# Rows of V in SBUF at a pitch of 512 bytes in place of 388: an attention kernel on one core

## The chip, the cores and the metric

The kernel runs on one core of one Trainium2 chip. The metric is the time of one execution on the device, in microseconds (us). Most executions of this kernel agree within 0.1%.

## The reference

An attention block whose output is multiplied by a gated feed-forward network. Only the attention matters here: 32 heads, 2048 queries, 2048 keys, 192 columns per head, all in bf16.

```python
scores = jnp.einsum("bhqd,bhkd->bhqk", q, k_cache) * (Dh ** -0.5)
p = _softmax(scores, axis=-1)
o = jnp.einsum("bhqk,bhkd->bhqd", p, v_cache)
# ... o @ wo, and x + s * silu(B(xn))
```

## The kernel before

V of one head is held in a tile of 128 partitions, with 16 rows of V in each. A row has 192 values, a column of ones (its product is the softmax's denominator) and one column of padding: 194 values of 2 bytes, 388 bytes. There are two such tiles, for alternate heads, and V is loaded a head ahead.

```python
vts = [vtp.tile([P, NKT, DH + 2], BF16, name=f"vt{i}") for i in range(2)]   # P=128, NKT=16, DH=192
...
def load_v(h, halves=(0, 1), queue=nc.sync):
    vt = vts[h % 2]
    for t in halves:
        ...                      # head 0 is loaded in two other halves
            nc.sync.dma_start(out=vt[:, :, 0:DH].rearrange("i (p t) d -> i p t d", t=2)[:, :, t, :],
                              in_=A_v_cache[0, h].rearrange("(p i t) d -> i p t d", i=P, t=2)[:, :, t, :])
...
for vt in vts:
    nc.vector.memset(vt[:, :, DH:DH + 1], 1.0)
```

The product with V comes in groups of 16 matmuls. A group belongs to one step p (0 to 7) and uses two rows of V, 2p (t = 0) and 2p + 1 (t = 1). Each pair (r = 0, 1) uses the two halves of the array's rows: in the trace its two matmuls (64 rows x 193 columns each) start 3.4 ns apart in the mean, and one is recorded with 243 ns. So a group is eight pairs: four with the even row, then four with the odd one.

```python
for t in range(2):
    for j in range(4):
        start = p == 0 and t == 0 and j % 2 == 0
        stop = p == NPAIR - 1 and t == 1 and j % 2 == 1
        for r in range(2):
            nc.tensor.matmul(obanks[r][:, j * 256:j * 256 + DH + 1],
                             lhsT=pT2[r * 64:(r + 1) * 64, t * 512 + j * P:t * 512 + (j + 1) * P],
                             rhs=vt[r * 64:(r + 1) * 64, 2 * p + t, 0:DH + 1], start=start, stop=stop)
```

`lhsT` is the stationary operand: beside the 16384 matmuls of this line the trace has 16384 weight loads of pT, of 94 ns each. `rhs`, the row of V, is the moving operand. Before each group stand three rounds of score matmuls (512 columns), and before every eight groups a projection of 20 matmuls. There are 1024 groups.

Of the kernel before, what the change touches and what calls it, by code (L numbers as in the profile page):

```python
# [11 lines left out]
BF16 = mybir.dt.bfloat16  # L12
# [3 lines left out]
P = 128  # L16
DH = 192
# [111 lines left out]
def _kernel_impl(  # L129
# [22 lines left out]
    NKT = SK // P  # L152
# [39 lines left out]
    vtp = att.enter_context(tc.tile_pool(name="vtp", bufs=1))  # L192
# [14 lines left out]
    xnS = xsp.tile([P, DC, SQ], BF16, name="xnS")  # L207
    x_all = fw.tile([P, WX], BF16, tag="xw", name="x_all")
    x_sb = x_all[:, 0:NQT * D].rearrange("p (t d) -> p t d", d=D)
    vts = [vtp.tile([P, NKT, DH + 2], BF16, name=f"vt{i}") for i in range(2)]  # L210
    loads = {}

    def load_x(g, t0=0, t1=4, queue=nc.sync):
# [547 lines left out]
@with_exitstack  # L761
def kernel(
    ctx: ExitStack,
    tc: tile.TileContext,
    A_x: bass.AP,
    A_k_cache: bass.AP,
    A_v_cache: bass.AP,
    A_wq: bass.AP,
    A_wo: bass.AP,
    B_x: bass.AP,  # L770
    B_w1: bass.AP,
    B_w3: bass.AP,
    B_w2: bass.AP,
    out: bass.AP,
):
    _kernel_impl(ctx, tc, A_x, A_k_cache, A_v_cache, A_wq, A_wo, B_w1, B_w3, B_w2, out)
# [30 lines left out]
```

## Time and profile before

The median was 1942.03 us over 3 runs (1940.68 to 1942.1). Six runs that include these have a median of 1941.95 us.

| what | before | where to read it |
|---|---|---|
| TensorE (PE) busy | 1929.6 of 1938.7 us | engines of the page |
| share of the V matmuls in the chain that ended last | 35% | chain of the page |
| V matmuls busy | 851.8 us | groups of the page |
| one V load, issue to landing | 5.6 us | DMA issues of the page |

These lines are from the page of the kernel before. A group's line gives engine, operation, output and inputs, shape, count; then its busy time in us and the mean of one in ns. A queue's line gives packets, MB and its share of the 16 DMA engines. An issue's line ends with the median from issue to landing in us.

```profile
span 1938.7 us, 59672 instructions
PE 1929.6 (100%) x27273; PEld 1318.5 (68%) x27281; DVE 654.0 (34%) x997; ACT 1180.2 (61%) x1278; POOL 282.6 (15%) x501
...
q1 hardware_dynamic: 371136, 125.32, 30.3%
...
PE 98%; DVE 1%; DMA 0%; ACT 0%; issue 0%; POOL 0%; DVEq 0%; ACTq 0%
...
L516 PE MATMUL obank<-vt,pT 64*128 64x193 bf16 x16384 | 851.8, 243 | 0.0
...
vt<-in_A_v_cache_dram SPq DMA_DIRECT2D x63, 384.0 KB, 5.6
```

TensorE is busy for 1929.6 of 1938.7 us, and the chain of waits runs through it for 98% of the span. Anything that makes the time shorter must make TensorE's own stream shorter. V loads are far from critical: they land in 5.6 us and are issued about 50 us before they are used (50.7 us in the median of the trace). One V matmul is recorded with 243 ns in the mean, but most pairs start 82.5 to 83.3 ns after the one before, so several overlap. What counts is the distance from one pair to the next.

### The profile page before, as it was taken

The page shows a single profiled execution, that of the slowest core. Times are in us where ns is not written, and L with a number is a line of the kernel's source. Part 1 is how long each engine was busy: PE and PEld are TensorE (multiplying, and loading weights), DVE is VectorE, ACT ScalarE, POOL GpSimd, SP SyncE. Part 2 cuts the span into 40 slices and gives each one's busy share as a digit, 9 for nine tenths or more (in the row PEclk, how much of TensorE's full clock was granted, in tenths as well). Part 3 has the DMA queues.
Part 4 walks back from the last instruction along what each step waited for, and adds up shares of the span by engine and source line. Part 5 has one row for each costly group of instructions (what it writes and reads, how often), then busy time and mean ns, then how long its engine had stood idle before and what let it go on. Part 6 is the DMA issues. An engine that isn't in the chain of part 4 may idle for free.

```text
span 1938.7 us, 59672 instructions
## 1 busy us (share of the span) xinstructions
PE 1929.6 (100%) x27273; PEld 1318.5 (68%) x27281; DVE 654.0 (34%) x997; ACT 1180.2 (61%) x1278; POOL 282.6 (15%) x501
## 2 busy tenths in 40 slices
PE   9999999999999999999999999999999999999998
PEld 6666666666666666666666666666666666577776
DVE  7333333333333333333333333333333334521111
ACT  6677676767676767776767777677767677210000
POOL 3111111111111111111111111111111110000000
PEclk9999999999999999999999999999999999999999
DMA  7643433323233433353434333434333220937772
GB/s 181 129 101 67 98 68 86 83 60 88 59 89 62 99 62 98 68 162 68 101 65 100 68 101 68 101 64 100 69 71 94 57 69 2 262 67 135 152 152 61
DMA packets 394643, 178.98 MB, mean 92 GB/s; under 512 B 341616, under 2 KB 382832, under 8 KB 394384
## 3 DMA queue, kind: packets, MB, share of 16 engines
q1 hardware_dynamic: 371136, 125.32, 30.3%
q0 software_dynamic: 19472, 45.71, 9.6%
q8 instruction: 215, 3.52, 0.8%
q10 hardware_dynamic: 3776, 4.06, 0.6%
q14 instruction: 44, 0.36, 0.1%
HBM read 52.82 MB, written 27.79 MB: 42 GB/s over the span
## 4 chain that ended last, share of the span: by engine, by line
PE 98%; DVE 1%; DMA 0%; ACT 0%; issue 0%; POOL 0%; DVEq 0%; ACTq 0%
PE obank L516 35%; PE st L487 33%; PE ps L424 14%; PE ps_s L111 11%; PE ps_f L727 3%; PE ps_gu L701 1%; PE st L488 1%; DVE stats L316 0%; PE ps L410 0%; DMA x_all<-in_A_x_dram 0%; DVE xn L346 0%; PE ps L391 0%; PE pst L354 0%; DVE mv L317 0%; PE pk L271 0%
## 5 line engine op out<-in xcount | busy, mean ns | idle before, releaser
L490 ACT ACTIVATE pT<-st 128x1024 bf16<-128x1024 f32 x1024 | 1046.2, 1022 | 251.8 <-PE st L488 236.2
L516 PEld LDWEIGHTS <-pT 64*128 64x128 bf16 x16384 | 713.7, 94 | 242.2 <-ACT pT L490 0.2
L516 PE MATMUL obank<-vt,pT 64*128 64x193 bf16 x16384 | 851.8, 243 | 0.0
L487 PE MATMUL st<-qC,KW 64*128 64x512 bf16 x2046 | 605.6, 376 | 0.1
L525 DVE COPY osum<-obank 128x772 f32<-128x772 f32 x128 | 123.0, 961 | 788.9 <-PE obank L516 788.9
L488 PE MATMUL st<-qB,KW 64*128 64x512 bf16 x1024 | 385.0, 376 | 0.0
L487 PE MATMUL st<-qA,KW 64*128 64x512 bf16 x1022 | 384.3, 376 | 0.4 <-ACT pT L490 0.3
L488 PE MATMUL st<-qC,KW 64*128 64x512 bf16 x1022 | 384.3, 376 | 0.0
L488 PE MATMUL st<-qA,KW 64*128 64x512 bf16 x1022 | 384.3, 376 | 0.0
L487 PEld LDWEIGHTS <-KW 64*128 64x128 bf16 x3068 | 278.0, 94 | 153.8 <-issue 2.1
L424 PE MATMUL ps<-xnT,W 64*128 64x512 bf16 x1280 | 297.2, 376 | 0.0
L424 PE MATMUL ps<-xnS,W 64*128 64x512 bf16 x1280 | 296.3, 376 | 0.0
L488 PEld LDWEIGHTS <-KW 64*128 64x128 bf16 x3068 | 278.0, 94 | 0.7 <-issue 0.6
L377 POOL DMA_DIRECT2D qC<-qA x124 | 65.4, 528 | 1285.6 <-DVE rl_all L532 1270.0
L430 ACT CAST qB<-ps 128x512 bf16<-128x512 f32 x131 | 76.7, 586 | 228.5 <-PE ps L424 222.9
L111 PE MATMUL ps_s<-wo_sb,oT 128*128 128x384 bf16 (+3 forms) x1535 | 208.8, 299 | 0.1
L424 PEld LDWEIGHTS <-W 64*128 64x128 bf16 x2560 | 122.9, 94 | 121.2
L111 PEld LDWEIGHTS <-oT 128*128 128x128 bf16 x1536 | 148.4, 98 | 60.4
L526 DVE TENSOR_TENSOR osum<-osum,obank 128x772 f32<-128x772 f32 x128 | 122.7, 958 | 13.4
L533 DVE TENSOR_TENSOR ostage<-osum,rl_all 128x768 bf16<-128x768 f32 x128 | 122.6, 958 | 4.4
L465 DVE SCALAR_TENSOR_TENSOR hT<-pt,qB 64x512 bf16<-64x512 bf16 x64 | 43.8, 684 | 199.5 <-ACT pt L464 199.5
L429 DVE CAST qA<-ps 128x512 bf16<-128x512 f32 x131 | 90.5, 691 | 25.2 <-PE ps L410 7.3
(84 smaller groups left out, 623.8 us busy)
## 6 DMA issues: line engine op xcount, KB each, us to landing
o_scr<-ostage SPq DMA_DIRECT2D x16, 1536.0 KB, 10.0
vt<-in_A_v_cache_dram SPq DMA_DIRECT2D x63, 384.0 KB, 5.6
qC<-qA POOLq DMA_DIRECT2D x248, 64.0 KB, 1.9
qC<-qB POOLq DMA_DIRECT2D x124, 64.0 KB, 2.3
wo_sb<-in_A_wo_dram POOLq DMA_DIRECT2D x1, 7680.0 KB, 35.3
W<-in_A_wq_dram POOLq DMA_DIRECT2D x32, 160.0 KB, 3.4
W<-in_B_w_dram POOLq DMA_DIRECT2D x32, 80.0 KB, 3.1
W<-in_A_wq_dram POOLq DMA_DIRECT2D x32, 80.0 KB, 2.9
```

What stands on the lines that cost most here:

```text
L111: nc.tensor.matmul(ps[:, 0:w], lhsT=oT[:, k, :], rhs=wo_sb[:, k, c0:c1], start=(k == 0), stop=(k == OC - 1))
L377: nc.gpsimd.dma_start(out=qC[0:64, half, :], in_=qAB[half][64:P, :])
L424: nc.tensor.matmul(ps[:, r * 512:(r + 1) * 512], lhsT=W[rows, j, :], rhs=xs[rows, j // 2, qs], start=(j == 0), stop=(j == 2 * DC - 1))
L429: a = nc.vector.tensor_copy(out=qAB[0][:], in_=ps[:, 0:512])
L430: b = nc.scalar.copy(out=qAB[1][:], in_=ps[:, 512:1024])
L487: nc.tensor.matmul(st2[:, 0:512], lhsT=ka, rhs=qa, start=r == 0 and nr == 3, stop=r == nr - 1)
L488: nc.tensor.matmul(st2[:, 512:1024], lhsT=kb, rhs=qb2, start=r == 0 and nr == 3, stop=r == nr - 1)
L490: nc.scalar.activation(out=pT2[:], in_=st2[:], func=ACT.Exp, scale=att_scale)
L516: nc.tensor.matmul(obanks[r][:, j * 256:j * 256 + DH + 1], lhsT=pT2[r * 64:(r + 1) * 64, t * 512 + j * P:t * 512 + (j + 1) * P], rhs=vt[r ...
L525: nc.vector.tensor_copy(out=osum[:], in_=ov[0])
L526: nc.vector.tensor_tensor(out=osum[:], in0=osum[:], in1=ov[1], op=ALU.add)
L533: nc.vector.tensor_tensor(out=ostage[:, qb * 4:qb * 4 + 4, hg * DH:(hg + 1) * DH], in0=osum[:, :, 0:DH], in1=rl.unsqueeze(2).to_broadcast( ...
```

## The change

Its intent is that each row of V starts on a round address, in the hope that aligned rows stream or land better. The columns in use are the same; only the padding grows. Nothing else is edited, and the order of instructions on all five engines stays the same.

```diff
-    vts = [vtp.tile([P, NKT, DH + 2], BF16, name=f"vt{i}") for i in range(2)]
+    vts = [vtp.tile([P, NKT, 256], BF16, name=f"vt{i}") for i in range(2)]
```

## The prediction

> **What bounds the kernel now.** TensorE. The page gives PE 1929.6 us busy in a span of 1938.7 us; the chain of work that ended last is 98% PE: 35% in the line that multiplies by V (obank<-vt,pT), 33% in the scores, 14% in the projections. The granted clock is 0.999. PE's largest wait is 2.8 us, once, at the start. The other engines have slack: VectorE waits 788.9 us for obank, ScalarE 236.2 us for st.
>
> **How near the V matmuls are to their floor.** They come in groups of 16: eight pairs, each on the two halves of the array's rows. In the timeline the group that starts at 1003.41 us is followed by the next matmul at 1004.08 us; from all records' start times a group takes 669.5 ns in the mean, 83.7 ns a pair. [...] 83.3 ns in the first four pairs, 82.5 in most later ones, 87.5 once in the middle. [...]
>
> **What the change does.** No instruction moves on any engine. V's rows start on multiples of 512 bytes from a tile's base; the tiles above in SBUF move up by 3968 bytes (16 rows x 124 bytes x 2 tiles), keeping their place within 128 bytes. The hope must be that aligned rows stream or land faster.
>
> - Reading. At 388 bytes the 16 rows of a tile start at 16 different offsets within 64 bytes, yet the group's time doesn't depend on the row: the medians for the eight pairs of rows (p = 0 to 7) are all 668 or 669 ns. [...] Expected: 0, at best -3 us.
> - Landing. A V load still consists of 384-byte runs; those take 22 ns in the median, between the 18 of 256-byte and 36 of 768-byte runs, so being unaligned costs nothing visible. A load lands in 5.6 us, issued about 50 us before its use; no PE wait names vt. Faster packets would not shorten the time.
> - The ones column: two memsets of 72 ns, with another step. Nothing.
>
> **Critical path share.** 35% of the span reads V; what the pitch could touch of it is about 0.
>
> **Predicted time.** 1941.5 us, 1935 to 1946 (8 in 10). Faster by over 2%: 0.01; within 2%: 0.97; slower by over 2%: 0.02.
>
> **What would show it.** Unchanged: the V matmuls' busy time (851.8 us) and mean (243 ns), 83 to 84 ns a pair; the chain's shares within a point; V loads landing in about 5.6 us; hardware queue 1 within a point of 30.3%; PE waits under 3 us.
>
> **What would make it wrong.** A power-of-two pitch could put two simultaneous accesses (a pair's reads, a read of V and a weight load from pT, a landing row) in each other's way all the time[...]: pairs well over 84 ns, the V share above 36%. Conversely, if all rows at 388 pay alike for what an aligned row doesn't, pairs fall to 82.5 ns or lower, worth some us. Moved tiles (xnS, W, q, pT) could change scores and projections.

(Cut are what no run of this case shows: a floor for the time of a pair, with the bound on any gain that was worked from it; a way of counting what the read of one row touches; and a half sentence on what 388 bytes do. The sum came to 1941.5 us, with 0 for reading, landing and the column of ones: about 0.5 us below the 1942.03 us of before. The first two cuts take two supports out of it, the bound and one of the two reasons for the 0 of reading; they take no other term. That 0 now stands on the group's time alone, which doesn't depend on the row (668 or 669 ns); "at best -3 us" was the author's estimate.)

## More of the kernel before

The next lines are from the chain that ended last, in order of time (start, us, what). They are two projections, which stand one at every eight V groups; 79 such stretches lie between the two.

```profile
252.21 2.16 PE ps L424 x20
...
1254.52 2.16 PE ps L424 x20
```

So one stretch of eight groups takes (1254.52 - 252.21) / 79 = 12.688 us. This is a finer measure than the span, since the start of the program varies from run to run (the projection at 1254.52 us here is at 1255.22 us in the repeat e1).

## The result, and the profile after

The changed kernel took 1939.39 us in the median of 6 runs (1938.82 to 1939.7), against 1941.95 us of before. The ratio was 0.9988, with a 95% interval of 0.9975 to 1.0001. Ratios here are the mean time of one kernel's runs over that of the other's of the same rounds, so they are not quite the ratio of the medians that are quoted. By the timed runs alone this is "the same", with a gain of about 2 us that the interval doesn't quite separate from zero.

The same parts of the page, after:

```profile
span 1937.4 us, 59668 instructions
PE 1927.5 (99%) x27273; PEld 1316.9 (68%) x27281; DVE 654.4 (34%) x997; ACT 1180.1 (61%) x1278; POOL 282.4 (15%) x501
...
q1 hardware_dynamic: 371136, 125.32, 31.5%
...
PE 98%; DMA 1%; DVE 1%; ACT 0%; SPq 0%; issue 0%; DVEq 0%; ACTq 0%
...
L516 PE MATMUL obank<-vt,pT 64*128 64x193 bf16 x16384 | 849.6, 243 | 0.0
...
vt<-in_A_v_cache_dram SPq DMA_DIRECT2D x63, 384.0 KB, 6.0
```

Two things moved. The V matmuls' busy time fell by 2.2 us, which is about the whole difference of the medians. V's loads became slower: 6.0 us and no longer 5.6, and queue 1 is busier with the same packets and bytes. The 1% of DMA in the chain is not from the change: it is the load of x at the program's start, and a repeat of the kernel before (e1 below) shows it too.

The chain in order of time, after:

```profile
252.66 2.16 PE ps L424 x20
...
1253.72 2.16 PE ps L424 x20
```

A stretch of eight groups takes (1253.72 - 252.66) / 79 = 12.672 us, so 16 ns less, 2 ns per group; 2 ns x 1024 groups are 2 us.

To see where in a group the 2 ns lie, I took the start times of all V matmuls from the trace and averaged, over the groups, the time from one pair's start to the next one's (the last: to the matmul that follows). Of 1021 groups the five that waited for something are left out.

| ns from each pair to the next | 1 | 2 | 3 | 4 | 5 | 6 | 7 | 8 | group |
|---|---|---|---|---|---|---|---|---|---|
| before (388) | 83.3 | 83.3 | 83.3 | 83.3 | 87.5 | 82.5 | 82.5 | 82.8 | 668.7 |
| after (512) | 83.3 | 83.3 | 83.3 | 83.3 | 83.4 | 83.3 | 83.3 | 83.3 | 666.7 |

Pair 5 is the first that uses the odd row of V. Before, it took 4.2 ns more, and the three after it 0.5 to 0.8 ns less each. After, all pairs are alike.

### The profile page after: what moved, and what is told of

Its sections match the earlier page's. It is cut to its first block, busy times and chain, and to the rows that moved or that the text cites. A ratio compares the mean times of both kernels' runs of the same rounds, so it can differ in the third digit from the quotient of the medians.

```text
span 1937.4 us, 59668 instructions
## 1 busy us (share of the span) xinstructions
PE 1927.5 (99%) x27273; PEld 1316.9 (68%) x27281; DVE 654.4 (34%) x997; ACT 1180.1 (61%) x1278; POOL 282.4 (15%) x501
## 3 DMA queue, kind: packets, MB, share of 16 engines
q0 software_dynamic: 19472, 45.71, 10.1%
## 4 chain that ended last, share of the span: by engine, by line
PE 98%; DMA 1%; DVE 1%; ACT 0%; SPq 0%; issue 0%; DVEq 0%; ACTq 0%
PE obank L516 35%; PE st L487 33%; PE ps L424 14%; PE ps_s L111 11%; PE ps_f L727 3%; PE ps_gu L701 1%; DMA x_all<-in_A_x_dram 1%; PE st L488 1%; PE ps L410 0%; DVE stats L316 0%; ACT KW L277 0%; PE pst L354 0%; ACT xnT L356 0%; DVE qA L429 0%; SPq L289 0%
```

## The experiments

There are two questions. What makes pair 5 long at 388 bytes? And what makes the loads slower at 512? Theory A was that the gain lies in the V matmuls themselves; its rival B, that 2 us are the noise of runs and chips. As A held, the next theories were about which property of the pitch counts: where a row starts (its alignment), how near it is to the row below, or how its start differs from that of the row used just before. Twelve runs were made, of which e1 and e2 repeat the two kernels and e9 repeats e7; all were correct. In the text, the "place" of a row is the remainder of its start in bytes, counted from the tile's start, when divided by 16. Where a recorded expectation has a mark of a cut, a clause is out that no run shows. The table at the end of this section has their numbers together.

### e1 and e2: both kernels again

There is no edit; both ran with five rounds on one chip.

> The kernel before, unchanged, against itself: the noise of the comparison. Theory A (the small gain of the change is in the V matmuls themselves: with rows at 388 bytes the second half of each group of 16 costs about 4.5 ns once, and less is given back) expects the same records as in the first profile: a mean of about 669.5 ns from the start of a V group to the next matmul, with the extra 4.5 ns at the second pair of the second half; ratio 1.000. Theory B (the 2 us between the kernels are the chip or the run, not the pitch) expects that this repeat differs from the first profile by as much as the changed kernel did. Packets of 384 bytes: if the mean of 28.5 ns belongs to the kernel it comes again; if it is the chip's, it moves.

> The changed kernel again. Theory A: 666.7 ns in the median from the start of a V group to the next matmul, all pairs alike at 83.3 ns, so faster by 2 ns x 1024 = 2 us, ratio about 0.999 with an interval that excludes 1. Theory B: ratio within 0.0005 of 1. The V loads' slower landing (6.0 us against 5.6, 384-byte packets 33 ns against 28.5 in the mean) comes again if the pitch of 512 bytes causes it.

Measured: 1941.24 us for the kernel before and 1939.44 us for the changed one, with ratios to the runs of before of 0.9998 (0.9984 to 1.0012) and 0.9990 (0.9976 to 1.0003). The V groups came out as the first time to 0.1 ns: 87.5 ns at pair 5 and 668.6 ns a group at 388, 666.7 ns at 512. The packets of 384 bytes of V again took 28.6 ns in the mean at 388 bytes and 33.3 ns at 512, and V landed in 5.6 and 5.8 us. So rival B falls: both effects belong to the kernels. The interval of the timed ratio didn't exclude 1, as A had hoped; the records show the 2 ns, the timed runs of this pair alone only suggest them. The busy time of the group, from the pages of e1 and e2:

```profile
L516 PE MATMUL obank<-vt,pT 64*128 64x193 bf16 x16384 | 851.8, 243 | 0.0
...
L516 PE MATMUL obank<-vt,pT 64*128 64x193 bf16 x16384 | 849.5, 243 | 0.0
```

### e3: a pitch of 392 bytes

```diff
-    vts = [vtp.tile([P, NKT, 256], BF16, name=f"vt{i}") for i in range(2)]
+    vts = [vtp.tile([P, NKT, DH + 4], BF16, name=f"vt{i}") for i in range(2)]
```

> Rows of V at a pitch of 392 bytes, so that each starts on a multiple of 8 bytes, every other one not on a multiple of 16. Theory A in the form that 8 bytes are what counts: groups of 666 to 667 ns as at 512 bytes, ratio about 0.999. Rival: 16 bytes[...] or 512 are needed; then the second half of a group[...] still costs the extra 4.5 ns and the group takes about 669 ns. Landing of V: at 5.6 us if the power-of-two pitch is what slows it, at 6.0 us if not.

Measured: 1940.98 us, ratio 0.9996 (0.9982 to 1.001). Pair 5 took 87.5 ns and a group 668.6 ns, as at 388. That each row starts on a multiple of 8 bytes doesn't help. The packets of V took 28.6 ns, as at 388, and V landed in 5.5 us.

```profile
L516 PE MATMUL obank<-vt,pT 64*128 64x193 bf16 x16384 | 851.9, 243 | 0.0
```

The busy time of the group, from the page of this run, is that of before, 851.8 us.

### e4: a pitch of 512 bytes, each row 4 bytes later

```diff
+    V0 = 2
-                nc.sync.dma_start(out=vt[:, :, 0:DH].rearrange(...      # and so for head 0
+                nc.sync.dma_start(out=vt[:, :, V0:V0 + DH].rearrange(...
-        nc.vector.memset(vt[:, :, DH:DH + 1], 1.0)
+        nc.vector.memset(vt[:, :, V0 + DH:V0 + DH + 1], 1.0)
-                                     rhs=vt[r * 64:(r + 1) * 64, 2 * p + t, 0:DH + 1], start=start, stop=stop)
+                                     rhs=vt[r * 64:(r + 1) * 64, 2 * p + t, V0:V0 + DH + 1], start=start, stop=stop)
```

> Pitch 512 bytes, but every row starts 4 bytes later, so that no row starts on a multiple of 8 bytes. If each row off 8 bytes cost something, all eight pairs would be long: groups well over 670 ns. If the cost is one of going from an aligned to an unaligned stream, it is paid once at the second pair of the group (4.5 ns) and the following pairs take 82.5 ns: groups of 665 to 670 ns. If alignment has no part in it and only a pitch of a power of two has, 666.7 ns as at 512. Time within 3 us of before in all cases. Landing of V as in the changed kernel if the pitch sets it, as before if alignment does.

Measured: 1939.30 us, ratio 0.9988 (0.9975 to 1.0002); all eight pairs 83.3 ns, 666.7 ns a group. V landed in 6.0 us, with packets of 33.1 ns.

```profile
L517 PE MATMUL obank<-vt,pT 64*128 64x193 bf16 x16384 | 849.4, 243 | 0.0
...
vt<-in_A_v_cache_dram SPq DMA_DIRECT2D x63, 384.0 KB, 6.0
```

Here no row starts on a multiple of 8 bytes, and the matmuls are as fast as with aligned rows. So the alignment of each row for itself has no part in the gain, and the loads are as slow as with aligned rows. What the change was meant for, aligned rows, is not what gave the 2 us.

### e5 and e6: the two loops of a group swapped, at 388 and at 512

```diff
-        for t in range(2):
-            for j in range(4):
+        for j in range(4):
+            for t in range(2):
```

The row of V now changes at each of the eight pairs (even, odd, even, ...), and no longer once.

> The kernel before (pitch 388) with the two loops of a V group swapped, so that the row of V changes at each of the eight pairs (seven changes) and no longer once. The group of eight pairs took 669 ns with one change and 666.7 ns where the change costs nothing (pitch 512). Theory C (each change from a row to the one that starts right behind its end costs something): about 2 to 4.5 ns per forward change, so a group of 675 to 685 ns and 6 to 16 us more in all. Theory D (the cost is paid once per group, whatever the order): 669 ns, time as before.

> The same swap with the pitch of 512 bytes. Theory C and D both expect 666.7 ns a group, since a change of row cost nothing at this pitch, and a time as the changed kernel's (1939.4 us). If this one is slower as well, changing the row costs something at any pitch and it was only hidden by the order. The difference to the run with 388 bytes is the worth of the pitch where the row changes often.

Measured: at 388 bytes 1947.72 us, ratio 1.0035 (1.0018 to 1.0051), so clearly slower than before; at 512 bytes 1939.47 us, ratio 0.9993 (0.9976 to 1.0009). The pairs of e5 take 83.3, 87.5, 82.5, 86.2, 82.5, 86.1, 82.5 and 86.1 ns, 676.8 ns a group; those of e6 are all 83.3 ns.

The busy time of the group, from the pages of e5 and e6:

```profile
L516 PE MATMUL obank<-vt,pT 64*128 64x193 bf16 x16384 | 857.7, 243 | 0.0
...
L516 PE MATMUL obank<-vt,pT 64*128 64x193 bf16 x16384 | 849.5, 243 | 0.0
```

The chain of e5 in order of time, to be read as that of before:

```profile
254.24 2.16 PE ps L424 x20
...
1260.24 2.16 PE ps L424 x20
```

A stretch takes (1260.24 - 254.24) / 79 = 12.734 us, 62 ns more than after. Theory C held and D fell: the cost comes with each change from the even row to the odd one. At 512 bytes a change of row is free (83.3 ns at each pair of e6). This pair of runs also amplifies the effect to where timing alone shows it: 1947.72 - 1939.47 = 8.3 us. The changes back, from the odd row to the even one, show no cost; those pairs take 82.5 ns, as do the pairs without a change of row that follow the long pair in the kernel before. In this run the rounds of score matmuls that follow also take 215.0 to 215.2 ns and not 215.8, so a part of the delay is made up afterwards: the groups grew by 10.1 ns against those of e6 (10.3 us in all), the time by 8.3 us.

### e7, e8 and e10: pitches of 448, 516 and 400 bytes

The edit of e3 with 224, 258 and 200 values in the tile's row. Each ran once.

> Pitch 448 bytes, a multiple of 64 but of no larger power of two; a row begins 62 bytes behind the end of the one below. If nearness to the last row's end is what cost the 4.5 ns (388: 2 bytes behind, 392: 6 bytes), the group takes 666.7 ns; if only a pitch that is a multiple of 128 or more avoids it, 669 ns. Landing of V and the mean of its packets: 5.6 us and 28.5 ns if the power of two slows them, 6.0 us and 33 ns if any wide gap does.

> Pitch 516 bytes, just off the power of two: rows start off multiples of 8 bytes as with 388, but 130 bytes behind the end of the row below. Nearness: 666.7 ns a group. Multiple of 64, 128 or 512 bytes needed: 669 ns. Landing of V: 5.6 us if the power of two is what slows it, 6.0 us if a wide gap does.

> Pitch 400 bytes: two rows of a group are at the same place within 16 bytes, but not within 32 or 64. Theory F ([...]388, 392 and 516 change that place, 448 and 512 don't, and a common offset of 4 bytes doesn't) expects no extra time[...] (666.7 ns a group, and no pair of 87.5 ns)[...]. A rival by which only the gap of bytes between rows counts (14 bytes here, 2 and 6 before) expects the same extra time as at 392.

(Theory F is that a V matmul takes longer when its row starts at another place than the row used just before. It left open by which number of bytes the place counts: 16, or 32 or 64, for which it expected the long pair at 400 bytes as well, about 669 ns a group.)

Measured: at 448 and 400 bytes all pairs 83.3 to 83.4 ns and 666.7 ns a group; at 516 bytes 85.8 ns at pair 5, then 82.5, 82.5 and 82.9, and 667.1 ns a group. The single times were 1938.91 (448), 1940.97 (516) and 1938.94 us (400). That of 516 is not the groups' alone: in its trace the first stretch of eight groups, at the program's start, took 1.1 us more than usual, and the median stretch is 12.675 us, 3 ns above the 12.672 of 512.

```profile
L516 PE MATMUL obank<-vt,pT 64*128 64x193 bf16 x16384 | 849.6, 243 | 0.0
...
vt<-in_A_v_cache_dram SPq DMA_DIRECT2D x63, 384.0 KB, 5.4
...
L516 PE MATMUL obank<-vt,pT 64*128 64x193 bf16 x16384 | 850.3, 243 | 0.0
...
vt<-in_A_v_cache_dram SPq DMA_DIRECT2D x63, 384.0 KB, 5.3
```

The first two lines are from the page of e10: the busy time is that of the changed kernel, the landing faster than both. The last two are from that of e8 (516). Nearness alone falls as a theory: at 516 bytes the odd row begins 130 bytes behind the end of the even one, and pair 5 is still long. "A power of two" falls too, with 448 and 400. What is left is theory F: 400, 448 and 512 are multiples of 16 bytes, so that the even and the odd row begin at the same place; 388, 392 and 516 are not.

Two results don't fit F as it is worded. In e5 the steps back to the even row change the place too, and cost nothing (82.5 ns). And rows have the same places at 516 as at 388, but pair 5 takes 85.0 ns for even p and 86.7 for odd p at 516, and 87.5 for every p at 388. There is also a rival that only e8 speaks against: if the tile is cut into pieces of 16 bytes from its start, the odd row begins at 388 and 392 bytes in the very piece in which the even row ended, and at 400, 448, 512 and 516 in a later one. A cost for that would explain e5's free steps back as well, but not the 2.5 ns at 516. It was not tested further.

### e12: a pitch of 388 bytes, but the two rows of a group eight rows apart

```diff
-                nc.sync.dma_start(out=vt[:, :, 0:DH].rearrange("i (p t) d -> i p t d", t=2)[:, :, t, :],
+                nc.sync.dma_start(out=vt[:, t * NPAIR:(t + 1) * NPAIR, 0:DH],
-                                     rhs=vt[r * 64:(r + 1) * 64, 2 * p + t, 0:DH + 1], start=start, stop=stop)
+                                     rhs=vt[r * 64:(r + 1) * 64, t * NPAIR + p, 0:DH + 1], start=start, stop=stop)
```

(The load of head 0 is cut accordingly.) This keeps the tile and the pitch of before, and takes away only the change of place: 8 x 388 = 3104 = 16 x 194.

> Pitch 388 as before, but the two rows of V of a group lie eight rows apart (3104 bytes, a multiple of 16) and no longer one (388 bytes); which keys they hold is unchanged, and so is the result. Theory F[...] expects no pair of 87.5 ns, 666.7 ns a group, and 1938.5 to 1939.6 us, as at pitches of 400, 448 and 512. Rival (the pitch itself must be a multiple of 16 bytes[...]): 669 ns a group and 1941 us, as before. Landing of V: the rows of one load now lie 388 bytes apart and no longer 776; near 5.5 us, off the critical path either way.

Measured: 1938.85 us, ratio 0.9986 (0.9972 to 0.9999). All pairs take 83.3 ns, a group 666.7 ns.

```profile
L517 PE MATMUL obank<-vt,pT 64*128 64x193 bf16 x16384 | 849.5, 243 | 0.0
```

The whole gain is had without a change of pitch, and here the interval just excludes 1. So it is not the pitch that counts, but the step between the rows that follow each other in a group. F's forecast held; but the rival of the shared piece forecasts the same here, since the odd row no longer begins where the even one ended.

### e11: the elements of a row 16 bytes apart

```diff
-                                     rhs=vt[r * 64:(r + 1) * 64, 2 * p + t, 0:DH + 1], start=start, stop=stop)
+                                     rhs=vt[r * 64:(r + 1) * 64, 2 * p + t, 0:DH + 8].rearrange("i (k o) -> i o k", o=8), start=start, stop=stop)
```

(At pitch 512. The column of ones is eight columns wide, and the last VectorE instruction puts the columns back in order.) Does it matter how far apart the elements lie that a moving operand reads one after the other?

> Pitch 512, result correct, but each V matmul reads its row in steps of 16 bytes (eight passes of 25 elements)[...]; 200 columns and no longer of 193 (eight columns of ones). [...] If a step within the row is free for the moving operand, [...]about 20 us more than the changed kernel, about 1960 us. VectorE's copies grow from 772 to 800 columns, 4% of 0.96 us, off the critical path.

(The 20 us and 1960 us were the author's estimate; one from the changed kernel's pairs is 83.3 x 200 / 193 = 86.3 ns a pair, so 691 ns a group and about 25 us more in all, 1964 us.)

Measured: 4394.48 us in one run, with the right result. A pair takes 356 ns where 86.3 is the estimate for 200 columns, and a group about 2.83 us.

```profile
span 4392.7 us, 59668 instructions
PE 4383.0 (100%) x27273; PEld 2606.3 (59%) x27281; DVE 772.2 (18%) x997; ACT 1188.2 (27%) x1278; POOL 282.5 (6%) x501
...
L516 PE MATMUL obank<-vt,pT 64*128 64x200 bf16 x16384 | 3579.3, 530 | 0.0
...
vt<-in_A_v_cache_dram SPq DMA_DIRECT2D x63, 384.0 KB, 4.0
```

The busy share of PE is 100%, as before: it doesn't tell these slow pairs from fast ones. The mean granted clock of this run was 0.851. In stretches of the run, a line being its time, then counts of busy us and instructions per engine, and near the end the granted clock:

```profile
1024.00:1070.00 46.00, 46.00 (x300) 27.16 (x298) 5.25 (x6) 13.97 (x15) 1.59 (x3) 1.00 0.35 85
1180.00:1195.00 15.00, 15.00 (x84) 10.08 (x82) 0.00 (x0) 3.07 (x3) 0.00 (x0) 0.50 0.01 1
```

The clock goes back and forth between 1.00 and 0.50. That isn't what makes the pairs long. The next lines are from the timeline of PE (start, us, what): first at a clock of 1.00 (the window 1205 to 1210 us has 1.00 as well), then at 0.50.

```profile
1205.77 3.01 PE L516 MATMUL obank<-vt,pT 64*128 64x200 bf16 x15
1208.29 0.39 PE L487 MATMUL st<-qA,KW 64*128 64x512 bf16 x1
...
1182.34 2.90 PE L516 MATMUL obank<-vt,pT 64*128 64x200 bf16 x14
1184.83 0.60 PE L487 MATMUL st<-qA,KW 64*128 64x512 bf16 x1
```

15 matmuls take 2.52 us to the next matmul at the full clock, and 14 take 2.49 us at half of it: 0.17 and 0.18 us each. So the array's clock doesn't set the pace here; the only edit to these matmuls that could is the step with which they read their rows. That is 356 / 200 = 1.78 ns for each element, where elements side by side took 83.3 / 193 = 0.43 ns. Whether a shorter step than 16 bytes would cost as much was not tested.

This run also bears on the second question, the slow loads. Its pitch is 512 bytes, yet its packets of V took 26.7 ns in the mean and V landed in 4.0 us. By its DMA records, 60 of the 62 loads after head 0 had at most 123 packets of other transfers beside them, and packets of 26.4 ns in the mean; the two that had 911 and 1625 beside them took 33.0 and 33.2 ns. In the changed kernel every load has at least 833. So the pitch of 512 bytes is slow only together with other traffic, as far as these loads tell.

### e9: the pitch of 448 bytes, timed

> Pitch 448 once more, with five rounds, as the candidate that beats both: V groups of 666.7 ns as at 512 bytes, V landing in 5.2 us (388: 5.6, 512: 5.8 to 6.0), 31 bytes in 128 of SBUF less than at 512. Since landing isn't on the critical path, the time should be the changed kernel's: 1939.0 to 1939.6 us. If landing mattered, it would be faster than 1939 us in the median.

(The size in this text is a slip: 448 bytes are 64 less than 512 for each row.) Measured: 1938.79 us (1938.69 to 1939.37), ratio 0.9989 (0.9976 to 1.0003); V groups 666.7 ns, V landing in 5.4 us. Against the changed kernel's 1939.44 us of e2 (other rounds) that is 0.03%, which these runs don't settle. It is as good with less memory and quicker loads; nothing here beat the changed kernel clearly.

Taken together, the timed runs do show the gain: all runs of kernels whose steps are multiples of 16 bytes (after, e2, e4, e6, e9, e12) lie between 1938.42 and 1940.39 us, and no run at a step of 388 or 392 bytes (before in all rounds, e1, e3, e5) is below 1940.61 us.

### All runs together

| run | step between the two rows, bytes | multiple of 16 | pair 5, ns | group, ns | mean packet of V, ns | us |
|---|---|---|---|---|---|---|
| before | 388 | no | 87.5 | 668.7 | 28.5 | 1941.95 |
| e1 | 388 | no | 87.5 | 668.6 | 28.6 | 1941.24 |
| e3 | 392 | no | 87.5 | 668.6 | 28.6 | 1940.98 |
| e8 | 516 | no | 85.8 | 667.1 | 28.8 | 1940.97 (once) |
| after | 512 | yes | 83.4 | 666.7 | 33.3 | 1939.39 |
| e2 | 512 | yes | 83.3 | 666.7 | 33.3 | 1939.44 |
| e4 | 512, rows 4 later | yes | 83.3 | 666.7 | 33.1 | 1939.30 |
| e7, e9 | 448 | yes | 83.3 | 666.7 | 27.2, 26.0 | 1938.91 (once), 1938.79 |
| e10 | 400 | yes | 83.3 | 666.7 | 27.7 | 1938.94 (once) |
| e12 | 3104, pitch 388 | yes | 83.3 | 666.7 | 28.6 | 1938.85 |
| e5 | 388, alternating | no | 82.5 | 676.8 | 28.9 | 1947.72 |
| e6 | 512, alternating | yes | 83.3 | 666.7 | 33.1 | 1939.47 |

In e5 the rows alternate, so that pair 5 is an even row there; its odd rows take 86.1 to 87.5 ns. The table leaves out e11, whose rows are read otherwise (356 ns a pair, packets of 26.7 ns at a pitch of 512, 4394.48 us once).

## Why the prediction was right or wrong

- The time was right: 1941.5 us was said, with 1935 to 1946, and 1939.39 us was measured. "Within 2%" had 0.97. The middle of the range came from the argument on reading, which missed the 2 us, and a range of 11 us can't tell the two apart.
- Right: TensorE bounds the kernel (98% of the chain), and a layout of V could give no more than a few us in these runs. An estimate from the trace of before: eight pairs at the 83.3 ns of its first four are 666.4 ns, 2.3 less than its 668.7, so 2.4 us over 1024 groups. 2 us came, and no layout that was measured went below 666.7 ns a group.
- Right: no instruction moved, the chain's shares for V (35%) and the scores (33%) stayed, no PE wait grew beyond 2.8 us, and slower loads (6.0 us and no longer 5.6) cost no time: none of these waits is for V.
- Mis-sized: "Reading. ... Expected: 0, at best -3 us". It was -2.0 us by the records (2.0 ns x 1024 groups). The step behind it, "the group's time doesn't depend on the row", was true, and so was that the alignment of each row is worth nothing (e4). What it missed is the relation of a row to the one before it. All rows at 388 bytes pay alike (87.5 ns for every p), and each group makes the same step of 388 bytes. The 87.5 ns "once in the middle" stood in the text without a cause; less what the three pairs after it gave back, it was the whole effect.
- Wrong in part: "if all rows at 388 pay alike for what an aligned row doesn't, pairs fall to 82.5 ns". They did pay alike, and it was worth 2 us, but the 82.5 ns were not the undisturbed pace but the making up after the long pair. Undisturbed pairs take 83.3 ns.
- Wrong: "V loads landing in about 5.6 us; hardware queue 1 within a point of 30.3%". They landed in 6.0 us (5.8 in the repeat), and the queue rose by 1.2 points. All four runs of the table with a pitch of 512 bytes have mean packets of V of 33.1 to 33.3 ns, 4 bytes later or not; the nine with another pitch have 26.0 to 28.9 ns. But e11, at 512 as well, has 26.7 ns where few other packets run beside the loads. Which part of the chip makes the packets slower at 512 was not tested. It stays open.
- The worry that a power of two might put simultaneous accesses of TensorE in each other's way didn't come true: 400, 448 and 512 give the same pairs, of 83.3 to 83.4 ns.

Shown is that a long pair at the change of row made the difference, and that it goes when the step between the rows is 400, 448, 512 or 3104 bytes. Open remain the mechanism behind the long pair, whether the place or the shared piece of 16 bytes counts at 388 and 392, why 516 bytes cost less than 388 (2.5 ns and 4.2) at the same places, and why only the step to the odd row costs and not that back (e5). In these runs the step from a score matmul's operand to a row of V shows no cost either, at any place of the row (the first pairs of e4 and of e12, whose rows start at places 0, 4, 8 and 12, take 83.3 ns).

## What to carry to other kernels

Where short matmuls follow one another with different rows as moving operand, try a step between these rows that is a multiple of 16 bytes: all four such steps of these runs (400, 448, 512 and 3104) were free, with 83.3 to 83.4 ns at the change of row, and the other three (388, 392 and 516) took 85.8 to 87.5 ns. That was worth 4 ns at a change of row, of which the next pairs gave back 2; it came to 0.1% of the time, and to 0.4% when the rows alternated at every pair. It is the step between rows used in turn that counts, not the alignment of each, so it can be had by placing rows in another order, or with 12 bytes of padding (400) as well as with 124 (512). Keep the elements of a row side by side: a moving operand with its elements 16 bytes apart made the same matmuls four times as long here (356 ns a pair, 86.3 by the estimate for elements side by side), at a PE busy share of 100%.
